# A 32-row form of the first expert layer, a cast in halves and a moved table in an attention and mixture-of-experts kernel

## Chip, cores and metric

The kernel runs on one core of a Trainium2 chip. The metric is device time in microseconds of one execution; of several runs the median counts. TensorE (PE) multiplies matrices, VectorE (DVE) and ScalarE (ACT) work on elements, GpSimd (POOL) and SyncE (SP) mostly start transfers.

## What is computed

Attention with a sigmoid instead of a softmax gives 3584 rows of 768 numbers. Each row is routed to the one of 8 experts whose embedding is nearest in angle, and goes through that expert's two-layer network:

```
attn = 1 / (1 + exp(-(scale * q k^T - log(S))));  x = attn @ v, as (3584, 768)
logits = xn @ en.T / tau;  expert_idx = argmax(logits);  gate_w = softmax weight of that expert
for e in range(8):
    mask = expert_idx == e
    h = maximum(x[mask] @ w1[e], 0)             # 768 -> 1024
    out[mask] = gate_w[mask, None] * (h @ w2[e])  # 1024 -> 768
```

## The kernel before

**Two halves of work.** The first part is the attention, a loop over 48 pairs of heads, in which rows are stored and routed as they come. The second part, the expert layers, works on *slots*: tiles of 128 rows of one expert. The routing counts rows per expert, rounds up to tiles, orders the experts by their number of tiles, the most first, and gives each a run of consecutive slots. Two early slots (-2 and -1) belong to the expert with the most rows in the first quarter. The loop at line 1121 is written for up to 39 slots; from slot 26 on a step is entered only if the slot is in use.

**Numbers.** Inputs and weights are split into a high and a low 16-bit part, and a product takes three matmuls: high by high, low by high, high by low (`L1_TERMS`, `L2_TERMS`, lines 207 and 208). Weights come from memory as 32-bit and are cast by `cast_block` (line 157): ACT makes the high part of a 128-row block (line 160), DVE the low part (line 163). The first matrix has six blocks, the second eight. There is one set of cast weights, so a new expert's first matrix can be cast only after the last first layer of the expert before, and the second matrix after its last second layer.

**A slot.** `gather` (line 1059, POOL) collects the slot's rows, `turn_rows` (line 1064, SP) transposes them, `layer1` (line 1078) multiplies, `hidden` (line 271) turns the result into the second layer's input: ReLU to the high part on ACT (line 276), the rest as low part on DVE (line 278, called the split below), both transposed by a transfer that SP issues (line 280). `layer2` (line 927) multiplies again, `evac2` takes the result out of PSUM with the gate as factor, `scatter` (line 1083, POOL) writes the rows.

**Short slots.** The last slot of an expert is often not full. A table `ci`, computed on DVE, holds a code for each slot: 0 full, 2 at most 64 rows, 4 unused. Each engine loads the code into a register when it first needs it for a slot (`code`, line 256), and branches. In the short form the array is split into two groups of 64 columns; the two halves of the layer's output run in them at once, half 0 in PSUM partitions 0 to 63 and half 1 in 64 to 127 of the same bank (`layer1_short`, line 221, and `layer2_short`). Then one ReLU and one split do for both halves; those of half 1 are skipped (`wide`, line 261).

**Order.** All engines follow the order in which the program is written. In step t:

```
layer1(t + 1) and its hidden          # line 1126
next weights' fetch, turn_rows(t + 3), gather(t + 4)   # rest_of_step; from step 25 on behind layer2(t)
cast(t + 2, 0)                        # first matrix, line 1149
layer2(t), evac2
scatter(t)
fetch(t + 2, 0), fetch(t + 1, 1)
cast(t + 1, 1)                        # second matrix, line 1162
```

`cast(u, which)` (line 986) loads a register that says whether slot u begins a new expert, and if so casts a matrix in two halves of three or four blocks, one right after the other. `fetch` (line 976) uses another part of `ci`, which says in which slot which expert's weights are fetched; that part of the table is computed in lines 1007 to 1033, just after the codes (lines 1002 to 1006) and before the last rows' sums. These sums (`later`, lines 1042 and 1043: an addition on DVE, line 473, and a square with sum on ACT, line 478) give the norms, from which the gates are made (`token_rest`, lines 860 to 910): DVE's product at line 894, PE's matmuls at line 898, DVE's sum at line 900.

## Time and profile before

| | us |
|---|---|
| median of 3 runs | 795.13 |
| lowest and highest | 793.67, 798.84 |
| the profiled execution's own time | 794.72 |
| its span, first to last instruction | 792.6 |

The profile's pages and the answers that the trace gives are read like this. Times are microseconds, those of single instructions nanoseconds. A group line has the line of the program, the engine, the operation, what it writes and reads, the shapes, the number of instructions, then busy time and mean duration, then the idle time before them and what ended it. PEld is TensorE's loading of weights, and its shape "128\*64" means 128 rows by 64 columns of the array. A timeline line has start, duration, engine, line, operation, a count, and in brackets how long the engine was idle before and what it waited for; a "q" behind an engine's name marks its instruction queue. A line of a stretch has from:to, its length, busy time and count of PE, PEld, DVE, ACT and POOL, then the granted TensorE clock (1.00 is full), the busy share of the transfer engines and GB/s. Lines of one instruction's durations give the lowest, the median and the highest in nanoseconds.

### The profile page before, as it was taken

The page shows a single profiled execution, that of the slowest core. Times are in us where ns is not written, and L with a number is a line of the kernel's source. Part 1 is how long each engine was busy: PE and PEld are TensorE (multiplying, and loading weights), DVE is VectorE, ACT ScalarE, POOL GpSimd, SP SyncE. Part 2 cuts the span into 40 slices and gives each one's busy share as a digit, 9 for nine tenths or more (in the row PEclk, how much of TensorE's full clock was granted, in tenths as well). Part 3 has the DMA queues.
Part 4 walks back from the last instruction along what each step waited for, and adds up shares of the span by engine and source line. Part 5 has one row for each costly group of instructions (what it writes and reads, how often), then busy time and mean ns, then how long its engine had stood idle before and what let it go on. Part 6 is the DMA issues. An engine that isn't in the chain of part 4 may idle for free. (4 is left out here: it accounts for less than half of the span.)

```text
span 792.6 us, 17627 instructions
## 1 busy us (share of the span) xinstructions
PE 764.8 (96%) x5847; PEld 375.2 (47%) x5847; DVE 376.4 (47%) x728; ACT 373.1 (47%) x551; POOL 200.9 (25%) x249
## 2 busy tenths in 40 slices
PE   6999999999999989899999999999999999999995
PEld 2334444443444434545555545555555555555553
DVE  3645467578778755943144111333144145444462
ACT  5777878777778762231134001422034134343451
POOL 2133343343334222204121211131131221222111
PEclk9999999999999999999999999999999999999998
DMA  9377897897989669959998998886899888999732
GB/s 232 85 192 182 195 221 209 226 270 197 251 212 250 187 133 143 232 140 220 225 211 182 243 151 181 217 222 192 195 283 265 235 179 209 249 256 262 112 79 46
DMA packets 237253, 157.97 MB, mean 199 GB/s; under 512 B 179020, under 2 KB 216374, under 8 KB 237104
## 3 DMA queue, kind: packets, MB, share of 16 engines
q1 hardware_dynamic: 228000, 122.11, 70.3%
q0 software_dynamic: 8688, 33.94, 14.2%
q8 instruction: 69, 1.13, 0.6%
q14 instruction: 80, 0.66, 0.3%
q10 hardware_dynamic: 416, 0.13, 0.1%
HBM read 95.51 MB, written 22.81 MB: 149 GB/s over the span
## 5 line engine op out<-in xcount | busy, mean ns | idle before, releaser
L218 PE MATMUL pss<-w,xt 128*128 128x512 f16 x900 | 198.5, 379 | 2.7 <-DMA xt<-stage 1.8
L230 PEld LDWEIGHTS <-hT 128*128 128x128 f16 x1296 | 126.2, 98 | 90.4 <-issue 3.4
L393 ACT ACTIVATE att<-pss,bias_s 128x896 f32<-128x896 f32 x144 | 139.7, 1005 | 33.5 <-PE pss L391 28.1
L1089 POOL DMA_INDIRECT out<-ob,six x60 | 62.8, 1047 | 331.2 <-ACTq L993 225.4
L218 PEld LDWEIGHTS <-xt 128*128 128x128 f16 x900 | 87.6, 98 | 107.0 <-issue 2.3
L420 PE MATMUL psa<-att,vt 128*64 128x448 f32 x576 | 125.2, 555 | 0.0
L276 ACT ACTIVATE hr<-pss 128x512 f16<-128x512 f32 x60 | 35.6, 596 | 181.9 <-PE pss L218 142.4
L278 DVE SCALAR_TENSOR_TENSOR hr<-pss,hr 128x512 f16<-128x512 f32 x60 | 41.1, 689 | 152.6 <-ACT hr L276 145.6
L163 DVE SCALAR_TENSOR_TENSOR w<-part,w 128x768 f16<-128x768 f16 (+1 forms) x98 | 97.7, 1065 | 32.7 <-ACT w L160 32.7
L230 PE MATMUL pso<-w,hT 128*128 128x384 f16 x672 | 111.5, 326 | 0.0
L230 PE MATMUL psa<-w,hT 128*128 128x384 f16 x624 | 103.7, 326 | 2.2 <-DMA hT<-hr 1.8
L391 PE MATMUL pss<-kq 64*128 64x448 f16 x864 | 99.8, 354 | 2.4 <-ACT att L393 1.3
L160 ACT ACTIVATE w<-part 128x768 f16 (+1 forms) x98 | 82.5, 921 | 14.2 <-DVEq L277 4.3
L358 POOL COPY pk<-qk 128x384 f32<-128x384 f32 x93 | 44.4, 505 | 145.1 <-PE ptr L370 71.0
L381 DVE SCALAR_TENSOR_TENSOR kq<-ptr,kq 128x448 f16<-128x448 f32 x96 | 59.8, 624 | 27.0 <-ACT kq L378 24.7
L391 PEld LDWEIGHTS <-kq 64*128 64x128 f16 x864 | 35.1, 95 | 75.7 <-issue 51.8
L420 PEld LDWEIGHTS psa<-att,vt 128*64 128x64 f32 x576 | 34.9, 136 | 60.3 <-issue 50.5
L380 DVE TENSOR_SCALAR kq<-ptr 128x448 f16<-128x448 f32 x70 | 43.4, 619 | 41.0 <-PE ptr L370 40.9
L445 DVE SCALAR_TENSOR_TENSOR xT<-psa,xT 128x384 f16<-128x384 f32 x96 | 32.9, 384 | 34.8 <-PE pss L391 23.7
L923 ACT ACTIVATE ob<-psa,own 128x384 f32<-128x384 f32 x16 | 9.3, 579 | 76.9 <-PE psa L230 50.0
L473 POOL TENSOR_TENSOR xf<-xrow 128x768 f32<-128x768 f16 x24 | 39.8, 1659 | 7.4 <-ACT xq L478 6.9
L1062 POOL DMA_INDIRECT stage<-xs,gix x31 | 32.4, 1047 | 27.3 <-issue 15.7
(227 smaller groups left out, 524.1 us busy)
## 6 DMA issues: line engine op xcount, KB each, us to landing
part<-in_moe_w SPq DMA_DIRECT2D x28, 1536.0 KB
qk<-in_q SPq DMA_DIRECT2D x48, 192.0 KB
qk<-in_k SPq DMA_DIRECT2D x48, 192.0 KB
vt<-in_v SPq DMA_DIRECT2D x48, 192.0 KB
xs<-xrow POOLq DMA_DIRECT2D x24, 384.0 KB, 6.0
stage<-in_moe_w SPq DMA_DIRECT2D x6, 512.0 KB
stage<-in_moe_w SPq DMA_DIRECT2D x8, 384.0 KB
tvv<-in_v SPq DMA_DIRECT2D x48, 32.0 KB
```

Source lines behind the costliest of these rows:

```text
L160: nc.scalar.activation(hi, s, AF.Copy, scale=SW)
L163: nc.vector.scalar_tensor_tensor(lo, s, SW, hi, op0=ALU.mult, op1=ALU.subtract)
L218: nc.tensor.matmul(ph[half][:, t % 2], xt[:, xi, kc, :], wts[wi][:, kc, half * HF:(half + 1) * HF], start=(n == 0), stop=(n == len(L1_TERM ...
L230: nc.tensor.matmul(po[d][:, :HD], hs[fc // 4][:, i, fc % 4, :], wts[wi][:, fc, d * HD:(d + 1) * HD], start=(n == 0), stop=(n == len(L2_TER ...
L278: nc.vector.scalar_tensor_tensor(hr[:, 1], ps, 0.0, hr[:, 0], op0=ALU.max, op1=ALU.subtract)
L358: en.tensor_copy(t.rearrange("p c h d -> p h c d"), qk[i][:, j])
L380: nc.vector.tensor_scalar(hi, x, SQK, None, op0=ALU.mult)
L381: nc.vector.scalar_tensor_tensor(lo, x, SQK, hi, op0=ALU.mult, op1=ALU.subtract)
L391: nc.tensor.matmul(ps[:, h, :S], x[r, ki, c * P:(c + 1) * P], x[r, qi, QC], start=(n == 0), stop=(n == 2))
L393: nc.scalar.activation(a, ps[:, :, :S], AF.Sigmoid, bias=bias_s, scale=1.0 / (8.0 * SQK * SQK))
L420: nc.tensor.matmul(accumulator(i)[h * D:(h + 1) * D, :S], vv[i][:, h, c, :], a[:, h, :], start=((i % 2 == 1 or i == 0) and c == 0), stop=( ...
L1089: ins = nc.gpsimd.indirect_dma_start(out.rearrange("n (h d) -> (n h) d", h=2), bass.IndirectOffsetOnAxis(ap=six[:, d, c:c + 1], axis=0), o ...
```

## The change

It has three parts.

**A form for up to 32 rows, in the first layer only.** The code table gets a value 3 for last tiles of at most 32 rows: `few` adds 1 to the 2 of short tiles. `layer1_quarter` uses four groups of 32 columns. Each half of the output is computed in two groups, which take turns over the 18 terms of the sum, so that PSUM holds two partial sums for each half, in partitions 0-31 and 32-63, and 64-95 and 96-127. In `hidden`, `summed` puts them together: ACT copies the second partial sum of each half to SBUF, in the buffer of half 1's ReLU, which such a slot doesn't use, DVE adds it to the first in PSUM, and then the ReLU follows. For all slots but the first, ACT and DVE get a branch for this, ACT a second one behind it. The second layer keeps the short form for codes 2 and 3.

**The second matrix cast in halves.** Blocks 0 to 3 are cast where all eight were, at the end of step t - 1; blocks 4 to 7 in step t, right behind layer1(t + 1) and its hidden.

**The fetch table later.** The lines that compute it become a function, called behind the `later` sums.

```diff
+    def layer1_quarter(t, xt):
+        for n, (kc, wi, xi) in enumerate(L1_TERMS):
+            for s in range(2):
+                o = s * HP + n % 2 * QP
+                nc.tensor.matmul(ph[0][o:o + QP, t % 2], xt[:, xi, kc, :QP], wts[wi][:, kc, s * HF:(s + 1) * HF],
+                                 start=(n < 2), stop=(n >= len(L1_TERMS) - 2))
...
+    def summed(t, ps, two, spans, act):
+        if t < 1:
+            return act()
+        with guard(ET.Activation, t):
+            with tc.If(code(ET.Activation, t) > 2) as br:
+                for to, at in spans:
+                    nc.scalar.activation(two[to], ps[at], AF.Copy)
+            with br.Else():
+                act()
+        with guard(ET.DVE, t):
+            with tc.If(code(ET.DVE, t) > 2):
+                for to, at in spans:
+                    nc.vector.tensor_tensor(ps[to], ps[to], two[to], op=ALU.add)
+        with guard(ET.Activation, t):
+            with tc.If(code(ET.Activation, t) > 2):
+                act()
+
+    EACH = [(slice(o, o + QP), slice(o + QP, o + HP)) for o in (0, HP)]
...
-        nc.vector.tensor_scalar(eh, eh, -float(HP), 1024.0, op0=ALU.is_gt, op1=ALU.mult)
-        nc.vector.scalar_tensor_tensor(eh, end, -1.0, eh, op0=ALU.add, op1=ALU.add)
+        few = bp1.tile([P, E], F32, name="few")
+        nc.vector.tensor_scalar(few, eh, -float(P - QP), None, op0=ALU.is_le)
+        nc.vector.tensor_scalar(eh, eh, -float(HP), 2.0, op0=ALU.is_le, op1=ALU.mult)
+        nc.vector.tensor_tensor(few, few, eh, op=ALU.add)
+        nc.vector.tensor_scalar(eh, end, -1.0, None, op0=ALU.add)
...
+        nc.vector.tensor_tensor(t6, t6, few.unsqueeze(1).to_broadcast(tab), op=ALU.mult)
...
-    def cast(u, which):
+    def cast(u, which, *halves_of):
...
-        for half in range(2):
+        for half in halves_of or range(2):
...
-        nc.vector.tensor_scalar(ca, hm[:, NE:], 2.0, -4.0, op0=ALU.mult, op1=ALU.add)
-        nc.vector.tensor_tensor(ca, ca, vd, op=ALU.mult)
+        nc.vector.scalar_tensor_tensor(ca, hc, -4.0, vd, op0=ALU.add, op1=ALU.mult)
...
         for f in later:
             f()
+    fetch_table()
...
             with tc.If(code(ET.PE, t) > 1) as br:
-                short()
+                if quarter:
+                    with tc.If(code(ET.PE, t) > 2) as few:
+                        quarter()
+                    with few.Else():
+                        short()
+                else:
+                    short()
...
             layer1(t + 1, xg_t.pop(t + 1))
+        cast(t, 1, 1)
...
-        cast(t + 1, 1)
+        cast(t + 1, 1, 0)
```

More of the change, by code (lines that the diff above doesn't have):

```diff
@@ L36 @@
 HP = P // 2
+QP = P // 4
 KQ = 2 * S
@@ L274, in hidden @@
         only = wide if half else guard
-        with only(ET.Activation, t):
-            nc.scalar.activation(hr[:, 0], ps, AF.Relu)
+        relu = lambda: nc.scalar.activation(hr[:, 0], ps, AF.Relu)
+        if half:
+            with wide(ET.Activation, t):
+                relu()
+        else:
+            summed(t, ps, ring("hr", 1, 1).rearrange("p i f -> p (i f)").bitcast(F32), EACH, relu)
         with only(ET.DVE, t):
@@ L966, in attn_moe_kernel @@
         nc.vector.scalar_tensor_tensor(eh, tl, -float(P), cnt, op0=ALU.mult, op1=ALU.add)
[L967 to L968 removed]
+        few = bp1.tile([P, E], F32, name="few")
[3 more added lines that the diff above has]
+        nc.vector.tensor_scalar(eh, end, -1.0, None, op0=ALU.add)
         t6 = bp1.tile(tab, F32, tag="t5", name="t6")
         nc.vector.tensor_tensor(t6, eh.unsqueeze(1).to_broadcast(tab), slot.unsqueeze(2).to_broadcast(tab), op=ALU.is_equal)
+        nc.vector.tensor_tensor(t6, t6, few.unsqueeze(1).to_broadcast(tab), op=ALU.mult)
+        hc = bp1.tile([P, MAXL], F32, name="hc")
+        nc.vector.tensor_reduce(hc, t6, axis=AX.X, op=ALU.add)
         hm = bp1.tile([P, NS], F32, name="hm")
         nc.vector.memset(hm[:, :NE], 0.0)
[L973 to L974 removed]
+        nc.vector.scalar_tensor_tensor(hm[:, NE:], hc, 1.0, vd, op0=ALU.is_gt, op1=ALU.mult)
     def fetch(u, n):
@@ L991, in cast, with fetch_table @@
         at = regs["c", u]
-        for half in range(2):
+        for half in halves_of or range(2):
             with tc.If(at < 2):
                 cast_part(2 * which + half, nc.s_assert_within(at, 0, 1))
-    man.enter_context(tc.manual_schedule(engines={ET.Activation, ET.SP, ET.Pool}))
-    with tc.manual_schedule(engines={ET.Activation, ET.SP, ET.Pool, ET.DVE}):
-        hidden(-1, 0)
-        layer1_full(-1, xte[1], 1, (6, 3 * NKC))
-        ci = bp1.tile([P, 4, MAXL], I32, name="ci")
-        hidden(-1, 1)
-        nc.vector.tensor_tensor(ca, ca, pr, op=ALU.mult)
-        nc.vector.tensor_scalar(ci[:, 0], ca, 2.0, None, op0=ALU.add)
-        nc.vector.tensor_scalar(ca, hm[:, NE:], 2.0, -4.0, op0=ALU.mult, op1=ALU.add)
-        nc.vector.tensor_tensor(ca, ca, vd, op=ALU.mult)
-        nc.vector.tensor_scalar(ci[:, 2], ca, 4.0, None, op0=ALU.add)
+    def fetch_table():
         pos = bp1.tile([P, E], F32, name="pos")
@@ L1033, in attn_moe_kernel @@
         nc.vector.tensor_scalar(ci[:, 1], ch, float(E - 1), None, op0=ALU.min)
+    man.enter_context(tc.manual_schedule(engines={ET.Activation, ET.SP, ET.Pool}))
+    with tc.manual_schedule(engines={ET.Activation, ET.SP, ET.Pool, ET.DVE}):
+        hidden(-1, 0)
+        layer1_full(-1, xte[1], 1, (6, 3 * NKC))
+        ci = bp1.tile([P, 4, MAXL], I32, name="ci")
+        hidden(-1, 1)
+        nc.vector.tensor_tensor(ca, ca, pr, op=ALU.mult)
+        nc.vector.tensor_scalar(ci[:, 0], ca, 2.0, None, op0=ALU.add)
+        nc.vector.scalar_tensor_tensor(ca, hc, -4.0, vd, op0=ALU.add, op1=ALU.mult)
+        nc.vector.tensor_scalar(ci[:, 2], ca, 4.0, None, op0=ALU.add)
         for f in wp:
@@ L1067, in turn_rows, with arms @@
         xg_t[t] = xt
-    def arms(t, full, short):
+    def arms(t, full, short, quarter=None):
         if t < 1:
@@ L1073, in arms @@
             with tc.If(code(ET.PE, t) > 1) as br:
-                short()
+                if quarter:
[3 more added lines that the diff above has]
+                        short()
+                else:
+                    short()
             with br.Else():
@@ L1078, in layer1 @@
     def layer1(t, xt):
-        arms(t, lambda: layer1_both(t, xt), lambda: layer1_short(t, xt))
+        arms(t, lambda: layer1_both(t, xt), lambda: layer1_short(t, xt), lambda: layer1_quarter(t, xt))
         for half in range(2):
```

2 lines of the change are left out of this document (removed).

## The prediction, made before the change ran

> Slots are the 128-row tiles of the expert layers, numbered t as in the main loop; L1(t) and L2(t) are TensorE's two layers of slot t. TensorE's order is L1(t+1), L2(t), L1(t+2), L2(t+1) and so on.
>
> **What bounds the kernel now.** I read the page first, then TensorE's timeline through the expert layers, then the timelines of ACT, DVE and SP where TensorE waits.
>
> ```profile
> span 792.6 us, 17627 instructions
> PE 764.8 (96%) x5847; PEld 375.2 (47%) x5847; DVE 376.4 (47%) x728; ACT 373.1 (47%) x551; POOL 200.9 (25%) x249
> ```
>
> PE is busy 96% of the span, so an edit counts only if it shortens PE's own work or moves one of PE's few waits. The groups by form give the work that the new form replaces in part:
>
> ```profile
> L224 PE MATMUL pss<-w,xt 128*64 128x512 f16 x216 | 24.5, 380 | 1.0 <-DMA hT<-hr 0.6 <-issue 0.4
> ```
>
> 216 short matmuls at 36 a slot are six short slots. PE's timeline shows when they run and where PE stops:
>
> ```profile
> 395.15 4.08 PE L224 MATMUL pss<-w,xt 128*64 128x512 f16 x36
> ...
> 467.56 2.76 PE L218 MATMUL pss<-w,xt 128*128 128x512 f16 x12 [1.83 <-DMA xt<-stage]
> ...
> 717.70 4.08 PE L224 MATMUL pss<-w,xt 128*64 128x512 f16 x36
> 721.71 7.97 PE L230 MATMUL pso<-w,hT 128*128 128x384 f16 x48
> 729.52 7.93 PE L218 MATMUL pss<-w,xt 128*128 128x512 f16 x36
> 737.38 4.09 PE L237 MATMUL psa<-w,hT 128*64 128x384 f16 x48
> 741.85 4.08 PE L224 MATMUL pss<-w,xt 128*64 128x512 f16 x36 [0.38 <-issue]
> 745.86 7.97 PE L230 MATMUL pso<-w,hT 128*128 128x384 f16 x48
> ...
> 754.73 7.50 PE L218 MATMUL pss<-w,xt 128*128 128x512 f16 x34 [0.47 <-DVE w L163]
> 762.16 4.09 PE L237 MATMUL psa<-w,hT 128*64 128x384 f16 x48
> ...
> 770.84 7.97 PE L230 MATMUL pso<-w,hT 128*128 128x384 f16 x48
> 780.85 5.77 PE L237 MATMUL psa<-w,hT 128*64 128x384 f16 x48 [2.03 <-DMA hT<-hr]
> ```
>
> From start to start a full L1 takes 7.8 us (729.52 to 737.38), a short L1 4.01 (717.70 to 721.71), a full L2 7.81, a short L2 4.1. Matmuls pair up in the short form: 36 in 4.01 us are 223 ns for two. Routing the reference's own inputs gives last tiles of 23, 32, 55, 4, 32 and 39 rows for the short slots 4, 16, 23, 26, 28 and 30. So four slots (4, 16, 26, 28) take the new form; L1(4) runs at 395.15, L1(26) at 717.70, L1(28) at 741.85. L2(30), at 780.85, lasted 5.77 us where the same 48 matmuls took 4.09 at 762.16, after the wait of 2.03:
>
> ```profile
> 781.00:784.00 3.00, 3.00 (x24) 1.75 (x22) 0.00 (x0) 0.00 (x0) 0.98 (x1) 0.60 0.37 134
> ```
>
> The seventh figure is the granted clock, 0.60: that wait also cost 5.77 - 4.09 = 1.7 us of slow clock.
>
> **Part 1, four column groups.** It removes no matmul: 36 a slot stay, in four column groups. If all four run at once, 36 x 223 / 4 = 2.0 us; if only pairs do, 4.0. No row shows a 32-column form. The nearest, the 64-column one, got 1.94 of its 2 (7.8 against 4.01), so I take 2.1 us: 1.9 saved a slot, bounds 0 and 2.0.
>
> The Trainium skill, "TensorE: Matmul & The Clock Gate", Part 3 (measured speedup), has 3.07 for four row groups and 2.38 for three column groups of a 512-wide matmul, which would make the new L1 some 2.5 us, an estimate, and the saving 1.5. The trace's 1.94 of 2 is nearer to ideal than that, so I keep my value.
>
> The price is paid on ACT and DVE. Before its ReLU a new-form slot runs two ACT copies and two DVE additions of 32x512. The trace has neither; the nearest rows are the ReLU and the split, of as many columns on four times the partitions:
>
> ```profile
> L276 ACT ACTIVATE hr<-pss 128x512 f16<-128x512 f32 x60 | 35.6, 596 | 181.9 <-PE pss L218 142.4
> L278 DVE SCALAR_TENSOR_TENSOR hr<-pss,hr 128x512 f16<-128x512 f32 x60 | 41.1, 689 | 152.6 <-ACT hr L276 145.6
> ```
>
> I take their 0.6 and 0.7 (bounds a quarter of that, by partitions, and the same). One copy lies beside an addition: 0.6 + 0.7 + 0.7 = 2.0 us later ReLU (0.5 to 2.0). Beside full slots that hides: L2(t-1), 7.8 us, lies between L1(t) and the next L1. At slot 4, ACT's first-matrix cast for slot 5 slips by these 2 us, and L1(5) starts 7.8 after L1(4); the casts were done well ahead:
>
> ```profile
> 402.49 6.90 DVE L163 SCALAR_TENSOR_TENSOR w<-part,w 128x1024 f16<-128x1024 f16 x6 [1.90 <-ACT w L160]
> 388.80 5.29 SPq L280 DMA_TRANSPOSE hT<-hr  x2
> ```
>
> First low block at 402.49 + 1.15 = 403.6 is 4.5 us after L1(4) ended (395.15 + 4.01); with 2.0 more it is 6.5, under 7.8. The second row is what may be late next: L2(3) would start at 395.15 + 2.1 = 397.2, and the transposes that feed it were issued until 394.09. I take 0.4 of loss there (0 to 1.9). Slot 4: -1.5; slot 16: -1.9.
>
> The new branches: the compare itself is short, register loads are what costs.
>
> ```profile
> L990 ACTq TENSOR_LOAD <-ci x29: 272/278/576, 388.4 to 781.4; - x29
> L993 ACTq COMPARE_BRANCH  x140: 18/45/55, 389.3 to 782.4; - x140
> ```
>
> The code register is already loaded once a slot for line 275; the change loads it one branch earlier, while ACT waits for PE. Added: two compares of 0.05 on ACT, one on DVE, under a 0.60 ReLU. I take 0.
>
> **Part 2, second matrix in halves.** The casts of slots 27 (second matrix) and 29 (first) as they are:
>
> ```profile
> 743.93 5.98 ACT L160 ACTIVATE w<-part 128x768 f16 x8 [1.78 <-SPq L983]
> 751.66 5.79 ACT L160 ACTIVATE w<-part 128x1024 f16 x6 [1.27 <-PE pso L230]
> ...
> 744.80 7.04 DVE L163 SCALAR_TENSOR_TENSOR w<-part,w 128x768 f16<-128x768 f16 x8 [5.01 <-ACT w L160]
> 753.45 6.90 DVE L163 SCALAR_TENSOR_TENSOR w<-part,w 128x1024 f16<-128x1024 f16 x6 [1.01 <-ACT w L160]
> ```
>
> A high block takes 0.75 (ACT), a low block 0.88 (DVE, beginning 0.87 after the high one); of the first matrix, a low block takes 1.15. The change keeps all of them, but blocks 4 to 7 now stand on ACT and DVE behind the ReLUs and splits of slot t+1, so they wait for L1(t+1). L2(t) starts at the same moment T and needs low block 4 at T + 4 x 0.98 + 0.33 = T + 4.2 (six matmuls a block). Expert switch to slot 24, T = 709.80:
>
> ```profile
> 709.80 2.44 PE L230 MATMUL psa<-w,hT 128*128 128x384 f16 x14
> ...
> 703.47 5.98 ACT L160 ACTIVATE w<-part 128x768 f16 x8 [0.76 <-DMA hT<-hr]
> 710.00 0.60 ACT L276 ACTIVATE hr<-pss 128x512 f16<-128x512 f32 x1 [0.56 <-PE pss L218]
> 711.01 0.60 ACT L276 ACTIVATE hr<-pss 128x512 f16<-128x512 f32 x1 [0.41 <-ACT hr L276]
> ```
>
> ReLUs end at T + 1.8; the gap of 0.41 holds the register load that moves ahead, so T + 1.4 to 1.8. A cast follows with 0 to 0.6 of entry, and low block 4 is done 0.87 + 0.88 = 1.75 later: T + 3.2 to 4.2. SP's queue is not moved past anything: its transposes of slot t+1 already waited for these splits, and its next weight fetch stands behind them. It just fits; 0 at the five switches with a full next slot (5, 12, 17, 21, 24), bounds 0 and 1.5 each (rival a).
>
> Slots 26 to 29 are the place where it doesn't fit: two experts of two slots follow each other, and casts set the pace already (the 0.47 at 754.73).
> With L1(26) 1.9 shorter, all of this moves 1.9 up, cast of slot 27 included (its release by SP's line 983 follows L1(27)): ACT 742.0, DVE 742.9. L1(28) ends at 742.0. Four high blocks to 745.0, copies to 746.2; low blocks to 746.4, additions to 747.8; ReLU to 748.4; 0.1 to 0.7 of entry; high block 4 at 749, low block 4 done at 750.3 to 750.9. L2(27), starting at 743.4 with low block 0, wanted it at 747.7: a wait of about 3 us. With 7.81 - 4.2 = 3.6 us left, L2(27) ends at 753.9 to 754.5. The first-matrix cast for slot 29 follows on ACT at 752.1 and on DVE at 753.2 to 753.9, its low block 0 is done 1.15 later, wanted two matmuls (0.43) into L1(29): start at 754.0 to 754.6, where 762.16 - 7.77 = 754.4 before. If the 3 us lower the clock as the 2.03 did, up to 1.3 is added; I count 0.9. So the shorter L1(26) and L1(28) bring nothing together: +0.8 (-0.4 to +2).
>
> At the end the halves help. ReLU and split of slot 30 stood behind eight casts:
>
> ```profile
> 769.24 7.04 DVE L163 SCALAR_TENSOR_TENSOR w<-part,w 128x768 f16<-128x768 f16 x8 [4.81 <-ACT w L160]
> 776.20 0.68 DVE L278 SCALAR_TENSOR_TENSOR hr<-pss,hr 128x512 f16<-128x512 f32 x1
> 786.72 0.58 ACT L923 ACTIVATE ob<-psa,own 128x384 f32<-128x384 f32 x1 [7.23 <-PE psa L237]
> 758.18 26.04 DMA out<-ob,six
> ```
>
> L2(30) began 780.85 - 776.88 = 4.0 after that split. Behind four low blocks the split is done at 769.24 + 4 x 0.88 + 0.69 = 773.5, so its transposes land by 777.5, before L2(29) ends at 778.7. Low block 4 of slot 29 follows at once, 774.4, needed at 770.84 + 4.2 = 775.0. So 2.03 and the 1.7 of slow clock go. What is late next: POOL's queue stood on the scatter before until 758.18 + 26.04 = 784.22, 2.5 us ahead of ACT's last output at 786.72, and that does not move fully with it. I take -3.0 (-1.5 to -3.9).
>
> The Trainium skill, "TensorE: Matmul & The Clock Gate", Part 1, lets the clock halve only after an idle window of about 3.4 us. The trace disagrees, 0.60 after 2.03 us, though 1.83 at 467.56 left the pace alone (12 matmuls in 2.76); by the page neither the end's 1.7 nor slot 27's 1.3 would hang on such a wait.
>
> **Part 3, fetch table behind row additions.** 22 small DVE operations move past the token products and four additions; three more come in ahead of slot -1's split, one of them as large as L970, two as small as L1008, and one small one goes:
>
> ```profile
> 319.45 0.48 DVE L970 TENSOR_TENSOR t<-eh,cst 128x312 f32<-128x312 f32 x1
> 323.07 0.21 DVE L1008 TENSOR_REDUCE pos<-low 128x8 f32<-128x64 f32 x1
> 328.83 0.18 DVE L1033 TENSOR_SCALAR ci<-ch 128x39 int32<-128x39 f32 x1
> 339.38 0.18 DVE L866 TENSOR_SCALAR rn<-rn 128x28 f32<-128x28 f32 x1 [2.54 <-ACT rn L865]
> 346.72 1.25 PE L898 MATMUL psr<-part,POH 128*128 128x82 f16 x28 [1.40 <-DVE part L894]
> 348.34 7.94 PE L218 MATMUL pss<-w,xt 128*128 128x512 f16 x36 [0.37 <-DVE own L900]
> ```
>
> The table, 5.9 us, now lies in the 2.54 that DVE waits for ACT's squares; less 0.48 + 0.2 of added operations, the gates come 1.5 to 1.8 earlier, over the 1.40 that L898 waits. The bound is 1.40 and the 0.37 before L1(1), 1.8 together; the product would then end just about when L1(0) does, so I take -1.1 (0 to -1.8). The table's first reader is SP, for slot 2's fetch at the end of step 0, behind L1(1): not held.
>
> **Sum.** -1.1 -1.5 -1.9 +0.8 -3.0 = -6.7, against the profiled 794.72: 788.0. The median shown is 795.13, 0.4 above it; I forecast 788.3, between the two. Own range 785.5 to 791. A measurement tells about 1% from no change here: 787.2 and 803.1 are the marks.
>
> **Rivals.** (a) The casts' second halves come late at every switch: if the branches cost ACT what the cast behind a short slot waited (1.27 above, twice), low block 4 arrives at T + 0.8 + 1.27 + 0.6 + 1.27 + 1.75 = T + 5.7 and PE stands 1.5 at five switches: 788.3 + 7.5 = 795.8, slower than before; it decides from T + 4.2 on. Against it: compares of 0.05. Chance 0.11. (b) Four groups run as two pairs: slots 4 and 16 give nothing, and 26 to 29 start unshifted, +2.5: -1.1 + 2.5 - 3.0 = -1.6, 793.1. Against it, 1.94 of 2. Chance 0.10. (c) All terms at their good ends (-1.8 -1.9 -1.9 -0.4 -3.9 = -9.9): 784.8; it needs the clock to stay up at slot 27 and no late transposes at slot 4. Chance 0.14. (d) The new form is never taken (a count over 32 on the chip): like (b). It needs several tokens to move; 0.02. The forecast keeps 0.63, of which about a third lies under 787.2. So faster by over 1% 0.35, within 0.60, slower 0.05. The range takes (c) and (b) in and leaves (a) out: 784.5 to 794.5.
>
> **What would show it.** Right: matmuls of 128x32, 144 of them, L1(4) near 2.1 us; a wait of some 3 us inside L2(27) on DVE's line 163 or ACT's 160; no wait before L2(30) and its 48 matmuls in 4.1; L898 without wait. Wrong: a new wait inside L2 at slots 5, 12, 17, 21 or 24; L1(16) near 4 us; L1(29) ending less than 43.5 us after L1(26) starts (44.5 before).

## The result and the profile after

The changed kernel took 804.1 us (median of 8 runs, 800.31 to 807.37) beside 797.38 for the kernel before in the same session (8 runs, 791.6 to 799.61): ratio 1.0103, 95% interval 1.0064 to 1.0141. It is slower by 1%, where 788.3 was forecast. A few executions of a kernel lie over 1.5% above its fastest; the ratios leave them out, and the traces of e1 and e13 are of such executions, so their waits are read for their place and not for their size. The profiled execution took 804.01 us. The first lines of its page:

```profile
span 801.9 us, 17894 instructions
...
PE 760.8 (95%) x5847; PEld 372.0 (46%) x5847; DVE 382.9 (48%) x738; ACT 378.3 (47%) x559; POOL 201.7 (25%) x249
```

TensorE's busy time fell by 4.0 us (764.8 to 760.8), yet the span grew by 9.3. So the change did shorten TensorE's work and gave it more to wait for. The groups by form show the new work:

```profile
L232 PE MATMUL pss<-w,xt 128*32 128x512 f16 x144 | 8.5, 380 | 0.4 <-issue 0.3
L225 PE MATMUL pss<-w,xt 128*64 128x512 f16 x72 | 8.2, 380 | 0.8 <-DMA hT<-hr 0.8
L291 DVE TENSOR_TENSOR pss<-pss,hr 32x512 f32<-32x512 f32 x8 | 5.6, 695 | 15.8 <-ACT hr L285 15.3 <-PE pso L238 0.4
L285 ACT ACTIVATE hr<-pss 32x512 f32<-32x512 f32 x8 | 4.7, 588 | 11.8 <-PE pso L238 11.8
```

144 matmuls of 32 columns are four slots, as forecast. TensorE's timeline around three of them and at the end (lines have moved: 232 is the new form, 225 the short one, 219 the full first layer, 238 and 245 the full and short second layer, 161 and 164 the casts on ACT and DVE, 1029 the branch around a cast):

```profile
576.28 2.13 PE L232 MATMUL pss<-w,xt 128*32 128x512 f16 x36
578.34 4.08 PE L238 MATMUL pso<-w,hT 128*128 128x384 f16 x24
583.93 0.48 PE L238 MATMUL pso<-w,hT 128*128 128x384 f16 x2 [1.52 <-ACTq L1029]
584.74 3.73 PE L238 MATMUL pso<-w,hT 128*128 128x384 f16 x22 [0.32 <-DVEq L1029]
...
598.93 1.98 PE L245 MATMUL psa<-w,hT 128*64 128x384 f16 x22 [0.39 <-DVEq L1029]
602.49 7.94 PE L219 MATMUL pss<-w,xt 128*128 128x512 f16 x36 [1.58 <-ACT ob L954]
...
728.69 1.62 PE L238 MATMUL pso<-w,hT 128*128 128x384 f16 x9 [1.78 <-issue]
730.49 3.73 PE L238 MATMUL pso<-w,hT 128*128 128x384 f16 x22 [0.17 <-DVEq L1029]
...
751.14 4.07 PE L238 MATMUL pso<-w,hT 128*128 128x384 f16 x24 [1.79 <-ACT w L161]
757.04 0.48 PE L238 MATMUL pso<-w,hT 128*128 128x384 f16 x2 [1.83 <-ACT w L161]
758.03 3.74 PE L238 MATMUL pso<-w,hT 128*128 128x384 f16 x22 [0.51 <-DVE w L164]
762.53 7.93 PE L219 MATMUL pss<-w,xt 128*128 128x512 f16 x36 [0.76 <-ACT w L161]
...
789.31 2.30 PE L245 MATMUL psa<-w,hT 128*64 128x384 f16 x26 [1.04 <-ACTq L1029]
792.00 1.98 PE L245 MATMUL psa<-w,hT 128*64 128x384 f16 x22 [0.38 <-issue]
```

L1(16) takes 2.06 us from start to start (576.28 to 578.34) where it took 4.01. But L2(15) behind it stops after 24 of its 48 matmuls for 1.52 and 0.32, until ACT and DVE have passed a cast's branch: all of the gain is gone. No expert switches there; the branch isn't even entered. From the starts of the layers, the time moved as follows (a minus is a gain against the kernel before):

| stretch | before | after | difference | forecast |
|---|---|---|---|---|
| L1(0) to L1(1): the fetch table | 10.95 | 9.37 | -1.6 | -1.1 |
| L1(4) to L2(4): form at slot 4 | 19.68 | 20.00 | +0.3 | -1.5 |
| L1(16) to L1(17): form at slot 16 | 11.82 | 12.03 | +0.2 | -1.9 |
| L1(17) to L1(23) | 89.84 | 92.33 | +2.5 | 0 |
| L1(23) to L1(26) | 39.38 | 41.27 | +1.9 | 0 |
| L1(26) to L2(28): slots 26 to 29 | 44.46 | 48.48 | +4.0 | +0.8 |
| L2(28) to the end of L2(30) | 24.46 | 23.59 | -0.9 | -3.0 |

Left out is the stretch from L2(4) to L1(16), -0.9: a wait for rows at slot 9, 1.83 before, was 0.45, and a wait of 0.30 came in L2(4). Left out too are L1(1) to L1(4), +0.3, and what follows TensorE's last matmul: the span goes on for 5.98 us before and 7.92 after, +1.9. From L2(28) to the end of the span the change so loses 1.1. The table's gain didn't reach L1(1) here (348.27 beside 348.34), since L1(0) itself began 1.5 us later; its start lies between 333.30 and 341.45 in the runs below, whatever the kernel. All this together makes the 9.3.

Two of the waits have a releaser that misleads. TensorE's own branches around the forms (line 1111) take 0.2 us as a rule; these two stand ahead of L1(18):

```profile
L1111 PEldq COMPARE_BRANCH  x2: 188/998/1807, 599.0 to 600.6; - x2
```

The second begins at 600.6 and lasts 1.81 us, to 602.4, and L1(18) starts at 602.49: its wait of 1.58, most of the +2.5, ends with this branch, while ACT's line 954 had ended at 601.5. In the same way a branch of 3.02 us from 748.1 on ends at 751.1, where L2(27) starts after 1.79; the first blocks of its weights were cast by 750.2.

So three kinds of wait are new in this trace. TensorE waits 4.9 us in sum until ACT or DVE have passed the branch of a cast (0.30 in L2(4), 1.84 in L2(15), 0.39 each in L2(16), L2(23) and L2(28), 0.17 in L2(25), 0.38 in L2(26), 1.04 before L2(30)). It waits 3.4 us behind its own two long branches, and 3.5 us in straight code on nothing that the profile shows (0.21 in L2(3), 1.08 in L2(22), 1.78 in L2(25), 0.38 in L2(30)). The casts that are really late cost 4.7 (L1(5), L2(27), L1(29)), where 0.5 stood before.

### The profile page after: what moved, and what is told of

Read it like the earlier page. It is cut to its first block, busy times and chain, and to the rows that moved or that the text cites. A ratio compares the mean times of both kernels' runs of the same rounds, so it can differ in the third digit from the quotient of the medians.

```text
span 801.9 us, 17894 instructions
## 1 busy us (share of the span) xinstructions
PE 760.8 (95%) x5847; PEld 372.0 (46%) x5847; DVE 382.9 (48%) x738; ACT 378.3 (47%) x559; POOL 201.7 (25%) x249
## 3 DMA queue, kind: packets, MB, share of 16 engines
q8 instruction: 78, 1.28, 0.7%
## 4 chain that ended last, share of the span: by engine, by line
issue 35%; DMA 12%; POOL 5%; POOLq 2%; DVE 0%; ACT 0%; ACTq 0%
DMA out<-ob,six 7%; DMA stage<-xs,gix 5%; POOL stage L1100 3%; POOL out L1133 2%; POOLq L266 2%; POOLq L1132 0%; POOLq L1133 0%; POOLq L1092 0%; POOLq L1100 0%; ACT hr L302 0%; DVE ob L1130 0%; DVE own L940 0%; DVE low_rows L939 0%; DVE low_rows L937 0%; DVE six L941 0%
## 5 line engine op out<-in xcount | busy, mean ns | idle before, releaser
L238 PE MATMUL psa<-w,hT 128*128 128x384 f16 x624 | 105.6, 329 | 4.2 <-DMA hT<-hr 2.6
```

The source lines that it names most:

```text
L238: nc.tensor.matmul(po[d][:, :HD], hs[fc // 4][:, i, fc % 4, :], wts[wi][:, fc, d * HD:(d + 1) * HD], start=(n == 0), stop=(n == len(L2_TER ...
```

## Experiments

Kernels that ran together share their runs of the kernel before: e1 to e4 (its median 795.79), e5 to e8 (794.05), e9 to e12 (794.5), e13 to e16 (796.88), e17 and e18 (795.18). Ratios are to it, with 95% intervals.

### The parts, one by one

e1_whole is the changed kernel with the second matrix cast whole again, e2_halves the kernel before with the cast in halves alone:

```diff
# e1_whole                          # e2_halves, on the kernel before
-        cast(t, 1, 1)              +        cast(t, 1, 1)
...
-        cast(t + 1, 1, 0)          -        cast(t + 1, 1)
+        cast(t + 1, 1)             +        cast(t + 1, 1, 0)
```

> The changed kernel with the second matrix cast whole again, at the old place. Gate theory: TensorE's second half of every L2(t) waits until ACT and DVE have passed the branches of the cast's second half, which stand behind ReLU and split of slot t + 1, whether or not there is a cast; taken away, the waits on the cast's branch inside L2 go (0.3 to 0.4 at each short L2, 1.8 at slots 15 and 25) and most of the new wait at slot 27: 4 to 9 us less than the changed kernel, 795 to 800. Code theory: the added branch arms make TensorE wait for instructions, and halves matter little: within 2 us of 804.

Measured: 807.56, ratio 1.0128 [1.0088, 1.0168].

> The kernel before with the cast in halves alone. Gate theory: 0.3 to 0.4 lost in each of six short L2, 2.1 together, none in full ones, and the last wait with its slow clock gone (up to 3.7): within 2 us of before, with waits on the cast's branch inside the short L2. Code theory: no arm is added, so no wait in L2, and the end's gain shows: 2 to 4 us faster.

Measured: 800.47, ratio 1.0086 [1.0048, 1.0124].

e3_quarter is the kernel before with the 32-row form alone, e4_table with the table moved alone:

> The kernel before with the form for up to 32 rows alone. Gate theory: four first layers of 2.06 instead of 4.01 us, 7.8 saved, less about 1.5 for the late first-matrix cast of slot 5 and what slots 27 to 29 give back (up to 4): 2 to 6 us faster than before. Code theory: TensorE stops for instructions behind the new arms, 1 to 2 us at several slots: no gain or slower.

Measured: 813.94, ratio 1.0227 [1.0169, 1.0284].

> The kernel before with the fetch table behind the row additions alone. Both theories: TensorE's wait of 1.4 before line 898's matmuls goes, 0 to 1.8 us faster, not told apart from no change by the times; the trace shows whether the first slot's layer starts earlier or the gain is lost before.

Measured: 793.04, ratio 0.9984 [0.9946, 1.0021].

The form is the worst part, twice as bad as the whole change. The halves cost something alone, more than either theory gave them, but taking them out of the changed kernel doesn't help either: in e1 the waits on the cast's branch are gone, and the rows of slot 27 come late instead (below). The parts don't add up: e1, the form and the table, loses 1% less than the form alone, and the table alone isn't worth that much; this isn't explained. The table is the only part that isn't a loss, though its gain can't be told from nothing by the times. The trace of e4 has no wait before the product at line 898 any more, and L1(1) starts 9.37 us after L1(0). All five kernels with the table moved have 9.37 to 9.39; of the fifteen with the table in its old place twelve have 10.95 to 12.00, and three (e3, e7 and e8, whose L1(0) came at 339 to 341) have 9.36 to 9.41; in two others it came as late, and they have 10.99 and 11.12. From e4:

```profile
335.01 7.93 PE L218 MATMUL pss<-w,xt 128*128 128x512 f16 x36
342.78 1.24 PE L898 MATMUL psr<-part,POH 128*128 128x82 f16 x28
344.38 8.07 PE L218 MATMUL pss<-w,xt 128*128 128x512 f16 x36 [0.36 <-DVE hr L278]
```

### Why the form's ReLU is so late

In the changed kernel L1(4) ends at 397.40, and then ACT's timeline reads:

```profile
401.01 1.19 ACT L285 ACTIVATE hr<-pss 32x512 f32<-32x512 f32 x2 [5.12 <-PE pso L238]
403.74 0.60 ACT L302 ACTIVATE hr<-pss 128x512 f16<-128x512 f32 x1 [1.54 <-issue]
405.54 2.95 ACT L161 ACTIVATE w<-part 128x1024 f16 x3 [1.20 <-DVEq L308]
```

The copies begin 3.6 us after L1(4), the ReLU 6.3 us after it, not 2.0 later than usual. The copies write the buffer of the other half's ReLU, and the transposes of the slot before read it too. e5_own is e3 with a buffer of their own:

```diff
-            summed(t, ps, ring("hr", 1, 1).rearrange("p i f -> p (i f)").bitcast(F32), EACH, relu)
+            summed(t, ps, halves[3][:, :HF], EACH, relu)
```

> The 32-row form alone, but the second partial sums are copied to a buffer of their own, a staging tile that the main loop doesn't use, instead of the buffer of half 1's ReLU. Buffer theory: the copies stood 1.9 to 2.6 us behind the layer's end because the transposing transfer of the slot before still read that buffer, and the ReLU of half 1 waited for DVE's branch; both go, 4 to 8 us less than with the shared buffer (813.9). Code theory (arms in every slot): within 2 us of it.

Measured: 807.08, ratio 1.0166 [1.0123, 1.021]. Its ACT timeline, with L1(4) ending at 398.61:

```profile
398.78 1.20 ACT L285 ACTIVATE stage<-pss 32x512 f32<-32x512 f32 x2 [1.54 <-PE pss L232]
401.52 0.60 ACT L302 ACTIVATE hr<-pss 128x512 f16<-128x512 f32 x1 [1.54 <-issue]
```

Now the copies begin 0.2 us after L1(4) and the ReLU 2.9. At slots 16 and 26 it is 0.2 again, where e3 has 1.9, 2.0 and 3.5 at the three slots. So a wait that goes with the shared buffer is shown; how long it is differs from run to run, since with the shared buffer the copies begin anywhere from 0.2 (e7 and e8 at slot 4) to 3.6 us behind the layer at these slots. That the transposes are what holds the buffer is argued, not shown. The rest of the 2.9 is the sum of 2 x 0.59 and 2 x 0.70 that don't overlap, and some 0.3 of hand-over. The loss is smaller than e3's by about 0.6 of a per cent, with intervals that overlap; most of it is elsewhere.

### The branches, never taken

In e6_never the limit is set so that no slot takes the form: all branches and TensorE's third arm stand in the program, and none is entered. e9_pe_arm has only TensorE's arm, e10_row_branches only those of ACT and DVE. All three keep the three added operations of the code table; so does e12 below, which isn't told from the kernel before, so these can't be what costs.

```diff
# e6_never, on e3_quarter
-        nc.vector.tensor_scalar(few, eh, -float(P - QP), None, op0=ALU.is_le)
+        nc.vector.tensor_scalar(few, eh, -float(P + 1), None, op0=ALU.is_le)
# e9_pe_arm, on e6_never
-            summed(t, ps, ring("hr", 1, 1).rearrange("p i f -> p (i f)").bitcast(F32), EACH, relu)
+            with guard(ET.Activation, t):
+                relu()
# e10_row_branches, on e6_never
-        arms(t, lambda: layer1_both(t, xt), lambda: layer1_short(t, xt), lambda: layer1_quarter(t, xt))
+        arms(t, lambda: layer1_both(t, xt), lambda: layer1_short(t, xt))
```

> The 32-row form alone with a limit that no slot meets, so that all arms and branches stand there and none is taken. Code theory: TensorE waits for instructions behind the longer arms (1 to 2 us at several short slots), and the shared buffer's waits stay: 3 to 9 us slower than before. Use theory (only taking the form costs): within 2 us of before.

Measured: 805.3, ratio 1.0152 [1.0107, 1.0197].

> The kernel before with TensorE's third arm (36 matmuls of 128x32) written at every slot but never taken; ACT and DVE have no added branch. Nothing of the result changes. Theory A (TensorE's longer program is the cost): as with all never-taken branches, 802 to 806 us, ratio 1.010 to 1.018, L2(22) waiting some 2 us on 'issue' behind slot 23's short form, and L1(27) waiting for its rows. Rival B (the branches ahead of ReLU and split on ACT and DVE are the cost): 793 to 797, ratio within 0.996 to 1.004, no wait at L2(22). If both carry a part, between 797 and 802.

Measured: 799.55, ratio 1.0071 [1.0034, 1.0108].

> The kernel before with only the added branches of ACT and DVE (copies and additions written at every slot, never taken); TensorE's program is as before. Theory A (TensorE's longer program is the cost): 793 to 797 us, ratio 0.996 to 1.004. Rival B (the branches on ACT and DVE are the cost, by delaying split, transposes, fetch and so the rows of slot 27): 801 to 806, ratio 1.009 to 1.018, with splits 0.3 to 0.6 us later after each L1 and a wait of 4 us before L1(27).

Measured: 804.96, ratio 1.0103 [1.0038, 1.0168].

So the form costs 1.5% without ever being used, and both theories hold a part: 0.7 for TensorE's arm, 1.0 for the branches. The branches are cheap, the place where they stand isn't. In e6's trace 2.2 us are lost from L1(23) to L1(26) and 6.9 from L1(26) to L2(28). The first loss goes with the arm, the second with the rows of slot 27, told further below. With the arm, TensorE often stands behind the short form of slot 23; e3's timeline there:

```profile
680.87 9.65 PE L238 MATMUL psa<-w,hT 128*128 128x384 f16 x48 [2.08 <-issue]
```

e1, e5, e6 and e9 wait 2.00 to 2.21 at the same place; the releasers named differ (nothing, a branch on ACT, a ReLU of slot 23 that L2(22) doesn't read). But in all five the wait ends with a long branch of TensorE's own: in e9 one of 4.43 us begins at 685.5, and L2(22) starts at 689.98; in e3 one of 4.29 us begins at 676.5, and L2(22) starts at 680.87. None of the kernels without TensorE's arm at that slot has the wait (before, e2, e4, e7, e8, e10 to e12, e14 to e18). The changed kernel has 1.08 a little later, and e13, whose TensorE program is that of e6, has none, so the program alone doesn't decide it. The durations of TensorE's own branch around the arms, in the kernel before, in the changed one and in e9:

```profile
L1073 PEldq COMPARE_BRANCH  x74: 65/208/1115, 348.0 to 784.4; - x74
```

```profile
L1111 PEldq COMPARE_BRANCH  x68: 65/218/3016, 348.0 to 792.1; - x68
```

```profile
L1109 PEldq COMPARE_BRANCH  x68: 65/216/4427, 349.6 to 796.4; - x68
```

A branch that usually takes 0.2 us takes up to 4.4 where the program is longer. Over all kernels the longest is 0.44 to 1.28 us without a third arm, 1.77 to 4.43 with one at two slots or more. The pages also count what queue q8 moves, which they call instructions: 69 packets with 1.13 MB in the kernel before and in e10, 78 with 1.28 MB in e9 and the changed kernel. So this traffic grows with TensorE's arms, even where none of their matmuls runs.

### The form without new arms, and where the code lies

e7_static4 writes the arms and branches only for slots 4, 16, 26 and 28, e8_static2 for 4 and 16:

```diff
+FEW = (4, 16, 26, 28)     # e8_static2: (4, 16)
...
+        if t not in FEW:
+            with guard(ET.Activation, t):
+                act()
+            return
...
-lambda: layer1_short(t, xt), lambda: layer1_quarter(t, xt))
+lambda: layer1_short(t, xt), (lambda: layer1_quarter(t, xt)) if t in FEW else None)
```

> The 32-row form alone, its arms and branches written only for slots 4, 16, 26 and 28, where these inputs use it; the other slots are as before. Code theory: most of the loss of the form in all slots goes, 5 to 12 us less than 813.9, and no wait for instructions behind slot 23. Use theory: within 3 us of 813.9.

Measured: 805.84, ratio 1.0103 [1.0046, 1.0159].

> The same for slots 4 and 16 alone; slots 26 and 28 run in the 64-row form. Place theory (the loss is made where two experts of two slots follow each other): 2 to 4 us faster than before, twice 1.95 less the late cast of slot 5. Code theory too, since the arms of the other slots are gone. If slots 4 and 16 bring nothing, both fall.

Measured: 801.57, ratio 1.0087 [1.0054, 1.012].

Fewer arms cost less: 1.0% in e7 where e3 has 2.3, which is what the theory of the longer code gave it. But they still cost, and e8, for which both theories gave a gain, is no better than e7. It waits 2.70 us on "issue" at L2(3), behind the form at slot 4, where a branch of TensorE's takes 3.94 us (it begins at 397.9, and L2(3) starts at 401.88), and 4.25 for the rows of slot 27. e12_replace2 puts the form in the place of the short one at slots 4 and 16, so that TensorE's program keeps its length; e16_pad is e12 with one arm at slot 10, a full slot, that is never reached:

```diff
# e12_replace2, on e8_static2 (and "> 2" becomes "> 1" in summed)
-lambda: layer1_short(t, xt), (lambda: layer1_quarter(t, xt)) if t in FEW else None)
+(lambda: layer1_quarter(t, xt)) if t in FEW else lambda: layer1_short(t, xt))
# e16_pad adds as last argument
+(lambda: layer1_quarter(t, xt)) if t in (10,) else None
```

> The 32-row form at slots 4 and 16 alone, in the place of their short form: no arm and no added level of branches on TensorE, whose program keeps its length; on ACT and DVE the copies and additions stand in the branch for short slots. The inputs put 23 and 32 rows there, so the result is the reference's. Theory A (arms and program length are the cost): the 1.9 us of each slot stay, L2(3) has no 'issue' wait, 790 to 793 us, ratio 0.995 to 0.998. Rival C (slots 24 to 27 stand on an edge, and an earlier or otherwise shifted arrival tips the rows of slot 27): a wait of 4 us or more before L1(27) all the same, 797 to 802, ratio 1.004 to 1.010.

Measured: 796.34, ratio 1.0022 [0.9985, 1.0058].

> The 32-row form in the place of the short form at slots 4 and 16, as run already, and one third arm on TensorE at slot 10 alone, which is a full slot, so the arm is never reached: all that changes before slot 16 is where TensorE's later code lies. Theory (the 1.84 us in L2(15) are a wait for instructions that hangs on where the code lies): the wait goes or is moved to another place, L2(15) runs in 7.8 us. Rival (the wait hangs on something else, such as the pace of the form itself): 1.8 us in L2(15) again, behind the same sixth matmul. Time 794 to 798 either way.

Measured: 797.81, ratio 0.999 [0.9952, 1.0028].

Without arms e8's loss can't be told from nothing any more, but no gain shows in the times. Of the two gains one stays in e12's trace: L1(4) gives its 1.95, but behind L1(16) TensorE stops, on nothing that the profile shows. The two timelines there, e12 and then e16:

```profile
577.22 2.13 PE L233 MATMUL pss<-w,xt 128*32 128x512 f16 x36
579.28 1.15 PE L239 MATMUL pso<-w,hT 128*128 128x384 f16 x6
582.27 7.00 PE L239 MATMUL pso<-w,hT 128*128 128x384 f16 x42 [1.84 <-issue]
```

```profile
576.35 2.13 PE L234 MATMUL pss<-w,xt 128*32 128x512 f16 x36
578.40 7.97 PE L240 MATMUL pso<-w,hT 128*128 128x384 f16 x48
```

In e16 only the place of TensorE's later code changed, and the wait is gone. In e3, e5, e7 and e8, which have the form at slot 16 and arms at other slots, it doesn't come either: all four take 9.87 us from L1(16) to L1(17), 1.95 less than before. So the wait hangs on where the code lies, as far as one trace of each kernel shows it. That it is a wait for instructions is what fits: 72 of them (36 matmuls and 36 weight loads) are through in 2.06 us, and what comes behind them wouldn't be there yet. No row shows an instruction arriving.

### The rows of slot 27

In e1, e3, e5, e6, e7, e8 and e10 TensorE stands 4.1 to 7.5 us, in e16 3.0, before L1(27), for the transposed rows. In all but e16, where L1(27) takes 7.94 us, a slow clock follows: it is 10.83 us long in e10, and the granted clock of that stretch is 0.52 (the seventh figure).

```profile
734.39 10.83 PE L219 MATMUL pss<-w,xt 128*128 128x512 f16 x36 [4.37 <-DMA xt<-stage]
```

```profile
734.50:740.50 6.00, 6.00 (x15) 2.10 (x15) 0.00 (x0) 0.00 (x0) 1.94 (x2) 0.52 1.14 313
```

SP's timeline shows where the rows' transposes come from, first before and then in e10, whose L2(24) start at 709.80 and 710.15:

```profile
712.01 3.38 SPq L280 DMA_TRANSPOSE hT<-hr  x2
716.13 0.39 SPq L173 DMA_DIRECT2D part<-in_moe_w  x1
717.96 2.18 SPq L1066 DMA_TRANSPOSE xt<-stage  x1
```

```profile
714.06 2.82 SPq L311 DMA_TRANSPOSE hT<-hr  x2
717.63 0.39 SPq L174 DMA_DIRECT2D part<-in_moe_w  x1
719.55 4.42 SPq L1101 DMA_TRANSPOSE xt<-stage  x1
```

SP's queue is a chain: transposes of slot 25's splits, then a fetch of weights (1536 KB), then slot 27's rows. In e10 the splits run 3.20 us after L2(24) starts and not 1.50; everything behind them slips, and the transposes themselves then take twice as long to issue. The chain begins a step earlier, with the transposes of slot 24 and the cast that follows them on ACT, first before and then in e10:

```profile
699.45 3.29 SPq L280 DMA_TRANSPOSE hT<-hr  x2
703.47 5.98 ACT L160 ACTIVATE w<-part 128x768 f16 x8 [0.76 <-DMA hT<-hr]
```

```profile
700.26 4.13 SPq L311 DMA_TRANSPOSE hT<-hr  x2
705.12 5.98 ACT L161 ACTIVATE w<-part 128x768 f16 x8 [2.06 <-SPq L1019]
```

The cast starts 0.73 us after SP has issued these transposes, in both, and in almost every other kernel with SP's order as before: it waits until SP has passed the branch of a fetch. Measured from L2(24), the cast is 1.30 us later in e10: the transposes begin 0.46 later, since the ReLU and the split of slot 24 stand behind one more branch and hand-over, and they take 0.84 longer to issue. Slot 25's split stands on DVE behind this cast, and its own hand-over adds some 0.4. All kernels in us after the start of L2(24):

| kernel | first split of slot 25 | transposes of slot 27 issued | wait before L1(27) |
|---|---|---|---|
| e2, e11, e15, e9, e4, e12, e18, before | 0.83 to 1.78 | 7.35 to 8.16 | none |
| after | 1.00 | 7.49 | none for rows |
| e16 | 2.18 | 8.27 | 3.00 |
| e17 | 2.31 | 8.43 | none |
| e5 | 2.26 | 8.54 | 4.57 |
| e7 | 1.75 | 9.10 | 7.31 |
| e6 | 3.13 | 9.29 | 4.14 |
| e10, e1 | 3.20, 3.08 | 9.40, 9.40 | 4.37, 7.01 |
| e8 | 1.87 | 9.46 | 4.25 |
| e3 | 2.92 | 10.14 | 7.50 |

Up to 8.2 the rows come in time, above 8.5 they never do. In e7, e8 and e16, whose slot 24 has no more hand-overs than before, its transposes begin as early as before and take 0.24 to 0.67 us longer to issue, and so the cast starts later. The table also says why the changed kernel is not worse than e3: with the cast in halves the splits stand ahead of four blocks, so its transposes go out at 7.49.

Three runs try this chain. e13_never_rows is e6 with the rows' transposes moved ahead of the fetch on SP, e14_rows the same edit on the kernel before:

```diff
+            if t + 3 < MAXL:
+                turn_rows(t + 3)
             if t:
                 fetch(t, 2)
             if t > 1:
                 fetch(t - 1, 3)
-            if t + 3 < MAXL:
-                turn_rows(t + 3)
```

> The kernel with all new branches, never taken, and one more edit: in each step SP issues the transposes of the rows of slot t+3 ahead of the weight fetches and not behind them. Theory (the delayed splits push these transposes over an edge at slot 27): they are issued 2 us earlier, near 7.4 us after L2(24) starts, L1(27) starts without its wait of 4.1 and without the 1.7 of slow clock behind it, and the time falls from some 804 to 797 to 800, ratio 1.003 to 1.008. Rival (the rows are late because their gather or the whole DMA is late, not because of their place in SP's queue): the wait stays at 4 us or moves to another slot, ratio 1.010 to 1.018.

Measured: 804.11, ratio 1.0106 [1.0072, 1.0141].

> The kernel before with that one edit alone (transposes of the rows ahead of the fetches). Theory: there nothing is late at slot 27, so no change, 793 to 797 us, ratio 0.996 to 1.003. Rival (the fetches are now the ones that come late): casts start later at the switches, waits on the casts inside L1 or L2, 797 to 802.

Measured: 799.33, ratio 1.0017 [0.9985, 1.0048].

The theory was half right. L1(27) doesn't wait for its rows in e13, but no clear gain comes of it (its interval overlaps that of e6): now the weights are late, since the casts wait until SP has passed the fetch, and the rows' transposes stand ahead of that:

```profile
749.56 4.08 PE L225 MATMUL pss<-w,xt 128*64 128x512 f16 x36 [0.39 <-issue]
757.38 0.48 PE L238 MATMUL pso<-w,hT 128*128 128x384 f16 x2 [3.74 <-ACT w L161]
758.37 9.31 PE L238 MATMUL pso<-w,hT 128*128 128x384 f16 x46 [0.51 <-DVE w L164]
```

e14 has the same at the same place, 2.65 and 0.51 inside L2(27), where the kernel before has nothing. Slots 24 to 29, four experts in six slots, have no slack on SP's queue: what is put first there pushes back the other. e14 also shows that the time of issue alone doesn't decide: it issues the transposes of slot 27 only 9.69 us after L2(24) starts, ahead of the fetch and not behind it, and the rows come in time. e17_held25 delays the split of slot 25 in the kernel before by two DVE operations and adds no branch; e18_held14 does so at slot 14.

```diff
+            if t == HELD and not half:     # 25, 14
+                for _ in range(2):
+                    nc.vector.tensor_scalar(halves[3][:, :HF], ps, 1.0, None, op0=ALU.mult)
```

> The kernel before with two more DVE operations (128x512 each, into a buffer that nothing reads) ahead of the first split of slot 25; no branch is added. Theory (the delay of the splits is what costs): this split moves from 1.5 to some 2.9 us after L2(24) starts, the transposes of slot 27 from 8.2 to 9.4 or later, L1(27) waits 3 to 5 us for them with slow clock behind it, 799 to 803 us, ratio 1.004 to 1.010. Rival (only the branches or the longer code do it): no wait at L1(27), 793 to 797, ratio 0.997 to 1.003.

Measured: 795.56, ratio 1.0022 [0.9989, 1.0056].

> The same two DVE operations at slot 14, beside full slots and far from a switch. Both theories: nothing waits for them, L1(27) starts without a wait, 793 to 797 us, ratio 0.997 to 1.003.

Measured: 794.4, ratio 0.9974 [0.9946, 1.0001].

e18 came out as expected. e17 is a miss: L1(27) has no wait. The casts of that execution started 0.5 us earlier, because slot 24's transposes took 2.78 us to issue and not 3.29; the split came at 2.31 and not at 2.9, and the transposes at 8.43, inside the gap of the table. So the run didn't reach the point where the theory says that it must cost. That a delay of 1.7 us alone makes the rows late is argued from the table and from e10, and not shown by itself.

### What is worth keeping

e11_half29 is e4 with halves at slot 29 alone, where the end's gain was forecast; e15_best is e11 with the form in the place of the short one at slots 4 and 16, as in e12.

```diff
+        if t == LATE:                      # 29
+            cast(t, 1, 1)
...
-        cast(t + 1, 1)
+        cast(t + 1, 1, *([0] if t + 1 == LATE else []))
```

> The kernel before with the fetch table moved and the second matrix cast in halves at slot 29 alone. By the prediction's own terms: -1.1 for the table and -1.5 to -3.9 at the end, so 788 to 791 us beside a kernel before of 794 to 796, ratio 0.993 to 0.997, no wait before L2(30). Rival (inside L2(29) TensorE waits for the branch of the late half on ACT and DVE, and L2(30) then for slot 30's transposes all the same): as the table alone, ratio 0.998 or more, with a wait of 1 to 2 us inside L2(29).

Measured: 791.99, ratio 0.9978 [0.994, 1.0015].

> The kernel before with the table moved, the second matrix cast in halves at slot 29 alone, and the 32-row form in the place of the short form at slots 4 and 16 (23 and 32 rows), without any added arm on TensorE. If the parts add up: 792 less 1.9 to 3.9, so 788 to 790 us, ratio 0.991 to 0.996. Rival (TensorE runs out of instructions behind the faster form, as L2(15) showed with 1.84): one of the two slots gives nothing, ratio 0.996 to 0.999, with a wait on 'issue' in L2(3) or L2(15).

Measured: 792.27, ratio 0.9915 [0.9875, 0.9955]. The end of its timeline:

```profile
768.73 8.27 PE L240 MATMUL pso<-w,hT 128*128 128x384 f16 x48
777.78 4.15 PE L247 MATMUL psa<-w,hT 128*64 128x384 f16 x48 [0.77 <-SPq L316]
```

Of the form's two gains of 1.95 little arrives in this execution. L2(15) waits 1.46 on "issue" here too, which leaves 0.3 from L1(16) to L1(17). Behind slot 4 the copies begin 2.8 us after L1(4), nearly as late as in the changed kernel, and L1(5) waits 0.50 and 0.67 on its casts, which leaves 0.5. The wait of 2.03 before L2(30) is down to 0.77, and its matmuls take 4.15 at full clock where they took 5.77. From L2(28) to the end of L2(30) e11 takes 21.68 us, 2.8 less than before. The span doesn't get all of it: it goes on for 7.70 us behind TensorE's end, where the kernel before has 5.98. All sixteen kernels with slot 29's second matrix cast whole have 5.98 to 7.26, the four with it in halves 7.70 to 7.93. e15 is the only kernel whose interval lies below 1: it is faster than the kernel before, and so than the changed one. That it is faster than e11 isn't shown: their medians are alike, 792.27 and 791.99, and the kernel before had 796.88 beside the one and 794.5 beside the other.

## Why the prediction was wrong

**The step that failed: "I take 0" for the new branches, and with it the halves counted at the expert switches alone.** The prediction priced the branches as compares of 0.05 us under a ReLU, and a cast in halves as nothing wherever no expert switches. In the changed kernel TensorE waits 4.9 us behind branches of casts, 3.4 behind its own long branches and 3.5 on nothing shown. The sum has no term for any of these. The runs show two things that were left out. A third arm at every slot, never taken, costs 0.7% (e9): TensorE's branches then take up to 4.4 us, and it stands some 2 us behind them (e3, e9). That such waits are for instructions is argued; that one of them hangs on where the code lies is shown by e12 against e16. And the branches of ACT and DVE cost 1.0% (e10): each puts ReLU and split later for SP's queue, on which the next cast, the next fetch and the rows of slot 27 stand in line. All of them together, never taken, cost 1.5% (e6), some 11 us. The prediction looked at SP's queue only for the halves ("not moved past anything") and at slots 26 to 29 only for the casts; it never priced the rows. In the changed kernel itself these don't come late; what costs there are the branches of the casts and TensorE's own.

**L1 of the new form** was right: 2.06 us where 2.1 was taken, and rivals (b), four groups in pairs, and (d), the form never taken, fall.

**The ReLU "2.0 us later"** was mis-sized: 2.9 us after L1's end with a buffer of its own (e5), 6.3 as built at slot 4, with the wait that goes with "the buffer of half 1's ReLU". The bound of 2.0 had taken only durations, no wait. So slot 4's first-matrix cast, expected in time by 1.3 us, came late (waits of 0.88 and 0.67 before L1(5)), and -1.5 became +0.3. In e3 the copies began 1.9 us after L1(4) and not 3.6, L1(5) didn't wait, and the stretch gave -1.4, as forecast; so the form alone doesn't always lose this.

**Halves, "0 at the five switches with a full next slot"** was right: L2(5), (12), (17), (21) and (24) have no wait on the casts, and rival (a) falls in its own form. What the prediction overlooked lies where nothing is cast at all. TensorE's second half of L2(t) waits until ACT and DVE have passed the cast's branch, and these stand behind the ReLU of slot t+1. Beside a short L2 that is 0.30 to 0.39 us (slots 4, 16, 23, 26, 28), and at L2(15), where the ReLU behind the form starts 4.7 us after L1(16) ends, it is 1.84. So Part 1 and Part 2 take each other's gain: the form alone gives -1.95 at slot 16 (e3), as forecast, and both together +0.2.

**Slots 26 to 29, +0.8**, became +4.0. The wait inside L2(27) was named rightly, 1.83 and 0.51 where about 3 was expected; the 1.79 ahead of it, which ends with TensorE's own branch, wasn't. L1(29) follows with 0.76. What was missing is L2(25), which stands 1.95 behind the form of slot 26, 1.78 of it on nothing that the profile shows, as in e12, so that L1(26)'s gain doesn't arrive.

**The end, -3.0**, and **the table, -1.1**, were right in kind: -2.8 (e11) and -1.6 by their own stretches on TensorE. What comes behind TensorE was underrated: to the end of the span e11 gains 1.1 against the kernel before and 2.3 against e18, which has the same end, and the bound was -1.5. In the changed kernel TensorE's end gives -0.9: 1.04 on the branch before L2(30), 0.38 inside it on nothing shown, 0.39 on the branch in L2(28) and 0.75 before L1(30) take the place of the 2.03.

**What stays open.** The rows of slot 27 come late also in e5, e7, e8 and e16, whose splits are late by less than 0.8 us. There it is the issue of transposes on SP that takes longer, slot 24's by a little and then slot 27's, 3.4 to 5.8 us where 2.2 to 3.1 is seen without a wait; why it does isn't settled. What a long branch of TensorE's waits for no row names. That the halves cost 0.9% alone isn't covered by e2's trace, whose execution was among that kernel's fastest (796.39 us, the median being 800.47).

## What to carry to other kernels

A branch that is never taken isn't free: ask which program it lengthens and who stands behind it, down to the transfer queues, above all where a stretch has no slack. A faster form is worth what the engine can be fed: its instructions, its buffers, and the engine that works behind it. When one kernel's program is unrolled and the tail tiles are known, replacing a form costs less than adding one.

## What the runs showed of the hardware

Four column groups of 32 give 3.8 times the full form (7.8 to 2.06 us for 36 matmuls), 0.95 a group. The Trainium skill, "TensorE: Matmul & The Clock Gate", Part 3, has 2.38 for three column groups, 0.79 a group; for four groups the measured pace decides.

A compare and branch on TensorE's queue took from 0.065 to 4.4 us (e9). The Trainium skill, "Advanced Engine Details and Errata" (Control Flow Timing), gives some 108 ns for one; the median here, 0.22, is twice that, and the longest is forty times that.

A copy of 32x512 on ACT takes 0.588 us and a 128x512 ReLU 0.597; an addition of 32x512 on DVE takes 0.695 and a 128x512 split 0.691: with a quarter of the partitions the work takes as long.

The slow clock didn't follow the length of a wait alone. At L2(22), waits of 2.08 (e3) and 2.21 (e9) were followed by 9.65 us for 48 matmuls, waits of 2.00 (e6) and 2.01 (e5) by 7.97; at L1(27) a wait of 3.00 (e16) was followed by 7.94 us for a first layer, at L1(20) a wait of 3.00 (e9) by 9.63. The Trainium skill, "TensorE: Matmul & The Clock Gate", Part 1, lets the clock halve after an idle window of some 3.4 us; the runs here show it after shorter waits, and not after each.
